# Linear attention beside a gated feed-forward, fp32 on one core: operands of the first key round loaded two feature blocks sooner, the first loads of w2 spread, and the last queries' sums put into rounds 1 and 2 of down

## The chip, the cores and the metric

The kernel runs on one core of a Trainium2 chip. The core has five engines that run beside each other, each with its own queue of instructions: TensorE (PE, with its weight loads apart as PEld), VectorE (DVE), ScalarE (ACT), GpSimd (POOL) and SyncE (SP). SP and ACT also ask for DMA transfers. The metric is the device time of one execution in microseconds (us), lower is better.

## The reference, cut to what matters

x is 2048 rows of 1024. It is normalized without parameters; two branches read the normalized xn. One is linear attention with 32 heads of 32, with a feature map of two softmaxes; the other is a gated feed-forward with 3584 features. Everything is fp32.

```python
xn = (x - mean) / sqrt(var + 1e-5)
q, k, v = split_heads(xn @ wqkv)
phi(t) = concat(softmax(t @ w_phi), softmax(-(t @ w_phi)))   # per head, over 32
kv = phi(k)^T v ;  z = sum over s of phi(k)
s = (phi(q) kv / (phi(q) z + 1e-6)) @ wo
g = silu((silu(xn @ w1) * (xn @ w3)) @ w2)
out = x + s * g
```

## The kernel before

**Products.** Every large matrix product is done by blocks with seven products in place of eight (Strassen's scheme in Winograd's form). The seven operands on one side are called A11, A12, S2, S1, S3, S4 and A22, those on the other B11, B21, T2, T1, T3, B22 and T4; the products run in the order of this list (ORDER), each named by its A operand. An fp32 operand is kept as a high part (a cast, ACT L93) and a low part (what the cast left over, DVE L94), and a product takes three passes (high x high, high x low, low x high). So a product of the gate and up, key and query stages is 12 matmuls of 128x512, and one of down 6.

**Stages.** Gate and up (L667) run over two halves of the rows (tb) and 28 feature blocks (f) of seven products (j = 0 to 6). Then come eight rounds for keys and eight for values (L930), eight query rounds (L1004; pos is their number, and the last of them is query_last), down (L1400), which multiplies the hidden features h by w2, and the output (L1554).

**Operands and loads.** The x operands of the key and query rounds (xo) lie in DRAM, each 512 KB per round, and reload() brings them back; wkv are the weights' operands, 2 MB each (op2B, op2T). The tiles of xo, the split weights of gate and up (bo) and the operands of down (hr, and the high and low parts af and as) share one pool of eleven buffers that is called q. Loads stand on SP's queue in the order in which the program writes them, mixed with the stores of h. The hidden features h are finished by DVE in each feature block and stored to h_d by SP. w2's operands go through a ring of 22 slots (load_b; the tiles are bo again), of which eight are there in the query rounds; two halves of 512 KB make one operand.

**Around the opening of down.** query_last computes the last pair of query blocks and prepares down's first operands between its products: first_parts makes A11 and A12 (af, cast and low part), and S2 (as2, which is made from sm, a sum of two parts of hr), second_parts makes the other four. The feature map of a query block is three steps (query_features): the maxima and the shifted values on DVE and GpSimd (ranged, L971 to L974), the exponential on ACT (raised, L977) that is stored by a transfer from ACT's queue (e_d), and the sums on DVE (summed, L982 to L984). What query_last doesn't finish it returns as a list of steps, and down runs it between its first products: a "piece" with number n is run behind product n of the rounds, 7 to a round.

**Down's rounds.** A round r works on one pair (kb, i): kb is a stretch of 512 features, i one of eight row groups. It runs A11, A12 and S2 of its own pair, mixed with S1, S3, S4 and A22 of the pair before. For kb = 0 the results are copied to acc by ACT (L1406) or added by DVE (L1414). A11 and S2 of one pair share a bank (bankb), which ACT has to have copied after A11 before S2 may start. gen1 is the generator that prepares the first operands of the next round, gen2 that of the other four of this one.

Of the kernel before, what the change touches and what calls it, by code (L numbers as in the profile page):

```python
# [28 lines left out]
def tile_kernel(ctx: ExitStack, tc: tile.TileContext, x, wkT, wqT, wv, wphi, wo, w1, w3, w2, out):  # L29
# [270 lines left out]

    in_order(ENG.PE, ENG.Activation, ENG.DVE, ENG.Pool, ENG.SP)
    ao, xs = {n: slot(0, j) for j, n in enumerate(ANAMES) if n in ("A11", "A12", "S2", "S1")}, []
    late_x = big.tile([P, 4, 2, 512], F, name="late_x", tag=f"big{HOMES[0][6]}")
    room_a = big.tile([P, 8, 4, P], F, name="room_a", tag=f"big{HOMES[0][5]}")
    room_b = big.tile([P, 8, 4, P], F, name="room_b", tag=f"big{HOMES[0][4]}")

    def load_tile(t, r):
        nc.sync.dma_start(r.rearrange("p u n -> p (u n)"), x[t * P:(t + 1) * P, :])
# [329 lines left out]
    def gate_up(step):  # L638
# [39 lines left out]
        def read():  # L678
# [37 lines left out]
            else:  # L716
# [11 lines left out]
                    del kept_banks[f]  # L728
                del banks[tb, f], bos[tb, f], bank
                h0 = u0 = u1 = h1 = None  # L730
            if last and tb:
                xo.update(reload(0, [ANAMES[0], ANAMES[1]] if j == 0 else ANAMES[j + 1:j + 2]))
            if last and (j < 5 if tb else 0 < j < 6):
                early.update(fetch(tb + 1, j + 1 + tb))
            if last and j == 6:
# [278 lines left out]
    def query_last(i, xo, wb):  # L1014

        bank, rho, q, feats, late = {}, small.tile([P, 2, 2, 16], F, name="rho"), {}, {}, []
        parts = first_parts(ahead.pop(0))

        def kept(n, pb):
            q[n] = work.tile([P, 512], F, name="q", tag="w")  # L1020
            nc.scalar.copy(q[n], pb)

        def added(n, pb, j, c, room):
            nc.vector.tensor_add(q[n], pb, q[n])
            feats[n] = query_features(i, j, c, q.pop(n), rho, nc.gpsimd, room, True)
            feats[n][0]()

        for b, an, bn in ORDER:
            pb = query_product(bank, b, an, bn, xo, wb)
            if an == "A11":  # L1030
                kept("00", pb)
                ahead[1] = load_h(0, 1)
            elif an == "A12":
                early = e_room()
                added("00", pb, 0, 0, early[:, 0])
                next(parts)
            elif an == "S2":
                kept("01", pb)
                feats["00"][1]()
                feats["00"][2]()  # L1040
                ready.append(next(parts))
                parts = second_parts(*ready[0])
            elif an == "S1":
                kept("11", pb)
                next(parts)
            elif an == "S3":
                added("11", pb, 1, 1, early[:, 1])
                next(parts)
            elif an == "S4":
                room = e_room()  # L1050
                added("01", pb, 0, 1, room[:, 0])
                feats["11"][1]()
                ready.append(next(parts))
                feats["11"][2]()
            else:
                feats["10"] = query_features(i, 1, 0, pb, rho, nc.vector, room[:, 1], True)
                feats["10"][0]()
        late.append(lambda: (feats["01"][1](), feats["01"][2]()))
        late.append(lambda: feats["10"][1]())
        late.append(lambda: (feats["10"][2](), rho_out(i, rho), feats.clear()))  # L1060
        return late

    def query_heads(i, first, xo, wb, steps):

# [70 lines left out]

    bos = {}

    def load_b(kb, n):
        n = BNAMES[n]
        for kk in range(2):  # L1140
            t = ring("bo")
            nc.sync.dma_start(t.bitcast(F), w2_d[kb][n][:, kk])
            bos[kb, n, kk] = t
# [50 lines left out]
    for c in range(3):  # L1194
# [5 lines left out]
        for pos, i in enumerate(order):  # L1200
            nxt, end = {}, pos + 1 == len(pairs)

            def steps():
                halves = []
                for j in range(7):
                    if not last:
                        wo_split(c, pos, j, halves)
                    if j == 0:
                        if pos in (3, 4) and not last:
                            wbn.update(fetch(3 + c, pos - 3))  # L1210
                        if not end:
                            nxt.update(reload(order[pos + 1]))
                        if last and 0 < pos < 5:
                            load_b(0, pos - 1)

                    if end and j in NEXT[c]:
                        wbn.update(fetch(3 + c, NEXT[c][j]))
                    if last and pos + 2 == len(pairs) and j == 5:
                        ahead[0] = load_h(0, 0)
                    yield  # L1220
# [230 lines left out]
    for k, do in enumerate((scale, scale, turn_e, turn_e)):  # L1451
        piece(7 * (50 + k // 2 * 2) + 5 + k % 2, lambda k=k, do=do: do(0, k % 2))
    old, banks, first, second = None, {}, ready[0], None
    for k, do in enumerate(late_features):
        piece(1 + 2 * k, do)
    late_features = None
    for r, new in enumerate(steps):
        kb, i = new or (NKB, 8)
# [2 lines left out]
            load_b(kb + 1, i - 2)  # L1461
        if r + 2 < len(steps) - 1:
            ahead[r + 2] = load_h(*steps[r + 2])
        if r == 2:
            late_rw.append(rwp.tile([P, 2, 2, 512], R, name="late", tag="rw"))
            room_z = rwp.tile([P, 2, D], F, name="room", tag="rw")
            zb, er = room_z[:, 0], room_z[:, 1]
# [12 lines left out]
        parts, bank = first, {}  # L1480
        if r and new:
            gen2 = second_parts(*parts)
        if r + 1 < len(steps) - 1:
            gen1 = first_parts(ahead.pop(r + 1))
        if kb and new:
            seed(i, bank, r)
        for m, (b, an, bn) in enumerate(TURN):
# [6 lines left out]
                    late_slots(bn)  # L1494
            if m < 3 and r and new:
                then = next(gen2)
            if m in (3, 4) and r + 1 < len(steps) - 1:
                first = next(gen1)
            if end and m in (1, 4) and 1 < i:
                gate(i - 2, m // 4)  # L1500
# [8 lines left out]
                do()  # L1509
        if new:  # L1510
            second = then if r else ready[1]
        old, banks = new, bank
    assert not pieces
    xrs = [slot_f("xr") for _ in range(2)]
# [130 lines left out]
```

## Time and profile before

| | |
|---|---|
| median of three runs | 2367.42 us (2367.08 to 2367.56) |
| the profiled execution, own time | 2366.58 us |
| its span in the trace | 2364.8 us |
| instructions | 37648 |
| DMA moved | 579.08 MB, mean 245 GB/s |

Times in the views are us from the start of the span. The page lists, for each engine, the time in which it was busy; PE was busy nearly all of the span, so the views that say more are the waits of PE, which list by cause each time PE stood still, and the timeline, where a row gives start, duration, engine, line and operation as "out<-in", with the idle time ahead of it and what ended that in brackets. The windows give the busy time of every engine, the clock that TensorE was granted (1 is full speed) and the use of the DMA engines in a stretch of time.

### The profile page before, as it was taken

How to read it: one execution, taken by the hardware profiler on the slowest of the kernel's cores; microseconds unless marked ns; L12 is line 12 of the kernel's file. 1: busy time of each engine (PE TensorE's matmuls, PEld its weight loads, DVE VectorE, ACT ScalarE, POOL GpSimd, SP SyncE). 2: the span in 40 equal slices, each digit the busy share in tenths (PEclk: the TensorE clock that was granted, in tenths of full speed). 3: DMA queues.
4: the chain of work that ended last, by engine and by line, in shares of the span. 5: the costliest groups of instructions: out<-in, count | busy, mean ns of one | idle time of the engine just before them, and what ended most of it. 6: DMA issues, size and time to landing. Idle time of an engine off the chain costs nothing.

```text
span 2364.8 us, 37648 instructions
## 1 busy us (share of the span) xinstructions
PE 2338.3 (99%) x14640; PEld 1916.5 (81%) x14640; DVE 1777.7 (75%) x2809; ACT 892.8 (38%) x1575; POOL 256.8 (11%) x213
## 2 busy tenths in 40 slices
PE   8999999999999999999999999999999999999999
PEld 6788877788888888888788888787888888888887
DVE  8877788875688888874566666777678888786775
ACT  6445444443355554443221222334433333352000
POOL 1000000000000000000000000331012222213562
PEclk9999999999999999999999999999999999999999
DMA  3556799997788988875978868986444553479763
GB/s 127 162 190 231 241 312 369 344 310 230 241 273 304 305 293 301 288 259 191 365 275 298 305 231 329 362 299 232 161 134 143 205 178 134 156 248 278 211 178 104
DMA packets 301490, 579.08 MB, mean 245 GB/s; under 512 B 24432, under 2 KB 156672, under 8 KB 298624
## 3 DMA queue, kind: packets, MB, share of 16 engines
q1 hardware_dynamic: 294976, 553.60, 69.3%
q10 hardware_dynamic: 6336, 23.07, 2.5%
q8 instruction: 115, 1.88, 0.3%
q14 instruction: 63, 0.52, 0.1%
HBM read 373.69 MB, written 202.91 MB: 244 GB/s over the span
## 4 chain that ended last, share of the span: by engine, by line
PE 95%; DMA 3%; DVE 1%; ACT 1%; issue 0%; SPq 0%; ACTq 0%
PE bankb L667 25%; PE bankb L1400 13%; PE bankc L667 12%; PE pm L1554 8%; PE bankb L930 7%; PE bankc L1400 6%; PE banka L667 6%; PE bankc L930 3%; PE bankb L1004 3%; PE banka L1400 3%; PE bankc L1004 2%; PE banka L930 2%; PE po L1539 1%; DMA xoA<-xo_d0A 1%; PE pkv L907 1%; PE banka L1004 1%
## 5 line engine op out<-in xcount | busy, mean ns | idle before, releaser
L94 DVE TENSOR_TENSOR bo<-rw,bo 128x512 fp32r<-128x512 f32 x329 | 226.1, 688 | 145.3 <-ACT bo L93 145.1
L1400 PE MATMUL bankb<-bo,as 128*128 128x512 f32 x960 | 236.3, 391 | 0.0
L1400 PEld LDWEIGHTS bankb<-bo,as 128*128 128x128 f32 x960 | 181.1, 189 | 37.7
L93 ACT CAST bo<-rw 128x512 fp32r<-128x512 f32 x329 | 202.3, 618 | 19.3 <-ACT wkvo L93 2.9
L667 PE MATMUL bankb<-op0S,bo 128*128 128x512 f32 x672 | 165.7, 396 | 4.5 <-ACT u L703 2.8
L667 PE MATMUL bankc<-op0S,bo 128*128 128x512 f32 x672 | 162.1, 390 | 0.0
L667 PE MATMUL bankb<-op1S,bo 128*128 128x512 f32 x672 | 161.3, 389 | 0.0
L667 PE MATMUL bankc<-op1S,bo 128*128 128x512 f32 x672 | 161.3, 389 | 0.0
L667 PE MATMUL bankb<-op0A,bo 128*128 128x512 f32 x672 | 159.3, 391 | 1.2 <-ACT op0A L765 0.8
L1554 PE MATMUL pm<-wos,oT 128*128 128x512 f32 x672 | 160.0, 393 | 0.0
L1400 PE MATMUL bankc<-bo,as 128*128 128x512 f32 x624 | 158.4, 389 | 0.0
L667 PE MATMUL bankb<-op1A,bo 128*128 128x512 f32 x672 | 157.9, 390 | 0.0
L667 PEld LDWEIGHTS bankb<-op0S,bo 128*128 128x128 f32 x672 | 125.6, 189 | 37.1 <-issue 5.3
L667 PEld LDWEIGHTS bankb<-op1A,bo 128*128 128x128 f32 x672 | 125.8, 188 | 28.1 <-DVE u L711 2.1
L667 PEld LDWEIGHTS bankb<-op0A,bo 128*128 128x128 f32 x672 | 125.4, 188 | 27.6 <-ACT op0A L765 1.1
L667 PEld LDWEIGHTS bankc<-op0S,bo 128*128 128x128 f32 x672 | 125.6, 188 | 27.3 <-issue 1.2
L667 PEld LDWEIGHTS bankc<-op1S,bo 128*128 128x128 f32 x672 | 126.2, 188 | 26.2
L667 PEld LDWEIGHTS bankb<-op1S,bo 128*128 128x128 f32 x672 | 126.2, 188 | 26.2
L1554 PEld LDWEIGHTS pm<-wos,oT 128*128 128x128 f32 x672 | 124.8, 188 | 27.4 <-DVE oT L1545 0.3
L1400 PEld LDWEIGHTS bankc<-bo,as 128*128 128x128 f32 x624 | 117.2, 188 | 24.4
L1414 DVE TENSOR_TENSOR acc<-bankb,acc 128x512 f32<-128x512 f32 x152 | 102.0, 685 | 32.7 <-PE bankb L1400 32.7
L718 ACT ACTIVATE h<-bankb 128x512 f32<-128x512 f32 x56 | 33.5, 598 | 239.7 <-PE bankb L667 239.5
(290 smaller groups left out, 4305.3 us busy)
## 6 DMA issues: line engine op xcount, KB each, us to landing
rw<-in_w SPq DMA_DIRECT2D x112, 512.0 KB, 4.9
hr<-h_d SPq DMA_DIRECT2D x56, 512.0 KB, 4.7
h_d<-h SPq DMA_DIRECT2D x108, 256.0 KB, 5.6
xoS<-xo_d0S SPq DMA_DIRECT2D x44, 512.0 KB, 7.2
xoS<-xo_d1S SPq DMA_DIRECT2D x44, 512.0 KB, 6.7
xoA<-xo_d0A SPq DMA_DIRECT2D x33, 512.0 KB, 5.3
xoA<-xo_d1A SPq DMA_DIRECT2D x33, 512.0 KB, 5.3
e_d<-eq ACTq DMA_DIRECT2D x32, 512.0 KB, 6.5
```

The costliest lines, as they stand in the source:

```text
L93: nc.scalar.copy(hi, src)
L94: (by or nc.vector).tensor_sub(lo, src, hi.bitcast(F))
L667: nc.tensor.matmul(bank[b], bos[tb, f][bn][:, w, k], ao[an][:, u, k], start=first and n == 0, stop=LAST[b] == an and n == 11, skip_group_c ...
L718: nc.scalar.activation(h1, bank["b"], AF.Silu)
L907: nc.tensor.matmul(pkv[sl, m], e[m // 4][:, (m % 4) * P + 32 * h:(m % 4) * P + 32 * h + 32], v[:, 4 * (m % 4) + h], start=first and m == 0 ...
L930: nc.tensor.matmul(bank[b], xo[an][:, u, k], wb[bn][:, w, k], start=an in ("A11", "A12", "S1") and n == 0, stop=LAST[b] == an and n == 11, ...
L1004: nc.tensor.matmul(bank[b], xo[an][:, u, k], wb[bn][:, w, k], start=an in ("A11", "A12", "S1") and n == 0, stop=LAST[b] == an and n == 11, ...
L1400: nc.tensor.matmul(bank[b], t[:, u, pos + k], bos[kb, bn, k][:, w], start=first and n == 0, stop=LAST[b] == an and n == 5, skip_group_chec ...
L1414: nc.vector.tensor_add(c, pb, c)
L1539: nc.tensor.matmul(po[32 * j:32 * j + 32, a, 64 * k:64 * k + 64], kvs[sl, j, c, k], et[sl, :, 4 * k + j], start=True, stop=True, skip_grou ...
L1554: nc.tensor.matmul(p, oTs[t, h][:, a, k], wos[c, 4 * h + k][:, b], start=n == 0, stop=n == 3 * ND - 1)
```

## The change

Four edits, and one exchange of lines:

- The x operands of the first key round are asked for in the last two feature blocks: A11, A12 and S2 in block 26 (products 4, 5 and 6), S1 and S3 with block 27's product 0, S4 and A22 with its products 3 and 4. Before, A11 and A12 were asked for with product 0 of block 27 and one more with each product after it.
- query_last makes the first operands of round 1, too (behind S4 and A22), and round 0 of down no longer does. The sums of query block 11 go from query_last into down; steps of the features move to pieces 1, 3 and 5 (round 0), 12 (round 1) and 19 (round 2, with the store of rho). The room that those features used is taken over for late w2 slots in round 4, not in round 2.
- The two halves of each of w2's first four operands are asked for at steps 2 and 5 of a query round, not both at step 0.
- Three rooms of the first stage are allocated in another order, so room_b has other addresses beside them.

```diff
--- before.py
+++ after.py
@@ -300,9 +300,9 @@
 
     in_order(ENG.PE, ENG.Activation, ENG.DVE, ENG.Pool, ENG.SP)
     ao, xs = {n: slot(0, j) for j, n in enumerate(ANAMES) if n in ("A11", "A12", "S2", "S1")}, []
+    room_b = big.tile([P, 8, 4, P], F, name="room_b", tag=f"big{HOMES[0][4]}")
     late_x = big.tile([P, 4, 2, 512], F, name="late_x", tag=f"big{HOMES[0][6]}")
     room_a = big.tile([P, 8, 4, P], F, name="room_a", tag=f"big{HOMES[0][5]}")
-    room_b = big.tile([P, 8, 4, P], F, name="room_b", tag=f"big{HOMES[0][4]}")
 
     def load_tile(t, r):
         nc.sync.dma_start(r.rearrange("p u n -> p (u n)"), x[t * P:(t + 1) * P, :])
@@ -728,8 +728,9 @@
                     del kept_banks[f]
                 del banks[tb, f], bos[tb, f], bank
                 h0 = u0 = u1 = h1 = None
-            if last and tb:
-                xo.update(reload(0, [ANAMES[0], ANAMES[1]] if j == 0 else ANAMES[j + 1:j + 2]))
+            if tb and f >= NF - 2:
+                xo.update(reload(0, {(0, 4): ANAMES[:1], (0, 5): ANAMES[1:2], (0, 6): ANAMES[2:3], (1, 0): ANAMES[3:5],
+                                     (1, 3): ANAMES[5:6], (1, 4): ANAMES[6:]}.get((f - NF + 2, j), ())))
             if last and (j < 5 if tb else 0 < j < 6):
                 early.update(fetch(tb + 1, j + 1 + tb))
             if last and j == 6:
@@ -1051,14 +1052,15 @@
                 added("01", pb, 0, 1, room[:, 0])
                 feats["11"][1]()
                 ready.append(next(parts))
-                feats["11"][2]()
+                parts = first_parts(ahead.pop(1))
+                next(parts)
             else:
+                ready.append(next(parts))
                 feats["10"] = query_features(i, 1, 0, pb, rho, nc.vector, room[:, 1], True)
                 feats["10"][0]()
-        late.append(lambda: (feats["01"][1](), feats["01"][2]()))
-        late.append(lambda: feats["10"][1]())
-        late.append(lambda: (feats["10"][2](), rho_out(i, rho), feats.clear()))
-        return late
+        return {1: lambda: feats["11"][2](), 3: lambda: feats["01"][1](), 5: lambda: feats["10"][1](),
+                7 + 5: lambda: feats["01"][2](),
+                14 + 5: lambda: (feats["10"][2](), rho_out(i, rho), feats.clear())}
 
     def query_heads(i, first, xo, wb, steps):
 
@@ -1135,9 +1137,9 @@
 
     bos = {}
 
-    def load_b(kb, n):
+    def load_b(kb, n, parts=range(2)):
         n = BNAMES[n]
-        for kk in range(2):
+        for kk in parts:
             t = ring("bo")
             nc.sync.dma_start(t.bitcast(F), w2_d[kb][n][:, kk])
             bos[kb, n, kk] = t
@@ -1210,9 +1212,8 @@
                             wbn.update(fetch(3 + c, pos - 3))
                         if not end:
                             nxt.update(reload(order[pos + 1]))
-                        if last and 0 < pos < 5:
-                            load_b(0, pos - 1)
-
+                    if last and 0 < pos < 5 and j in (2, 5):
+                        load_b(0, pos - 1, (j // 3,))
                     if end and j in NEXT[c]:
                         wbn.update(fetch(3 + c, NEXT[c][j]))
                     if last and pos + 2 == len(pairs) and j == 5:
@@ -1451,8 +1452,8 @@
     for k, do in enumerate((scale, scale, turn_e, turn_e)):
         piece(7 * (50 + k // 2 * 2) + 5 + k % 2, lambda k=k, do=do: do(0, k % 2))
     old, banks, first, second = None, {}, ready[0], None
-    for k, do in enumerate(late_features):
-        piece(1 + 2 * k, do)
+    for k, do in late_features.items():
+        piece(k, do)
     late_features = None
     for r, new in enumerate(steps):
         kb, i = new or (NKB, 8)
@@ -1461,7 +1462,7 @@
             load_b(kb + 1, i - 2)
         if r + 2 < len(steps) - 1:
             ahead[r + 2] = load_h(*steps[r + 2])
-        if r == 2:
+        if r == 4:
             late_rw.append(rwp.tile([P, 2, 2, 512], R, name="late", tag="rw"))
             room_z = rwp.tile([P, 2, D], F, name="room", tag="rw")
             zb, er = room_z[:, 0], room_z[:, 1]
@@ -1480,7 +1481,7 @@
         parts, bank = first, {}
         if r and new:
             gen2 = second_parts(*parts)
-        if r + 1 < len(steps) - 1:
+        if 0 < r < len(steps) - 2:
             gen1 = first_parts(ahead.pop(r + 1))
         if kb and new:
             seed(i, bank, r)
@@ -1494,7 +1495,7 @@
                     late_slots(bn)
             if m < 3 and r and new:
                 then = next(gen2)
-            if m in (3, 4) and r + 1 < len(steps) - 1:
+            if m in (3, 4) and 0 < r < len(steps) - 2:
                 first = next(gen1)
             if end and m in (1, 4) and 1 < i:
                 gate(i - 2, m // 4)
@@ -1509,6 +1510,9 @@
                 do()
         if new:
             second = then if r else ready[1]
+            if r == 0:
+                first = ready[2]
+                ready.clear()
         old, banks = new, bank
     assert not pieces
     xrs = [slot_f("xr") for _ in range(2)]
```

In the changed kernel line numbers from L735 on are one to four higher. How the order moves on SP's queue at the first key round. xo are the x operands, op2T and op2B the weights' operands. From A12's load on, before:

```order
L630 DMA xoA_9715<-xo_d0A_88 128x1024
L170 DMA op2T_9717<-wkv_d1T_110 128x4096
L630 DMA xoS_9737<-xo_d0S_89 128x1024
L170 DMA op2T_9739<-wkv_d1T_111 128x4096
L623 DMA h_d_6_70<-h_9581 128x4x128
L630 DMA xoS_9759<-xo_d0S_90 128x1024
L170 DMA op2T_9761<-wkv_d1T_112 128x4096
L630 DMA xoS_9778<-xo_d0S_91 128x1024
L170 DMA op2B_9780<-wkv_d1B_113 128x4096
L630 DMA xoS_9795<-xo_d0S_92 128x1024
L170 DMA op2T_9797<-wkv_d1T_114 128x4096
L630 DMA xoA_9813<-xo_d0A_93 128x1024
```

and after the change:

```order
L630 DMA xoA_9679<-xo_d0A_88 128x1024
L630 DMA xoS_9699<-xo_d0S_89 128x1024
L630 DMA xoS_9719<-xo_d0S_90 128x1024
L630 DMA xoS_9721<-xo_d0S_91 128x1024
L170 DMA op2T_9723<-wkv_d1T_110 128x4096
L170 DMA op2T_9743<-wkv_d1T_111 128x4096
L623 DMA h_d_6_70<-h_9581 128x4x128
L170 DMA op2T_9763<-wkv_d1T_112 128x4096
L630 DMA xoS_9780<-xo_d0S_92 128x1024
L170 DMA op2B_9782<-wkv_d1B_113 128x4096
L630 DMA xoA_9797<-xo_d0A_93 128x1024
L170 DMA op2T_9799<-wkv_d1T_114 128x4096
```

S2, S1 and S3 (xoS, of d0S_89, 90 and 91) stand ahead of the first two weights' operands now; S4 and A22 one weight operand sooner than before.

How it moves on ACT's queue at the opening of down. as<-s is a cast of round 0's second operands, af<-hr and as<-sm those of round 1's first ones, COPY acc<-bankb the copy of a product of down, and eq and e_d are the exponentials of the query features and their store. Before:

```order
L93 CAST as<-s_14353 128x512
L1406 COPY acc<-bankb 128x512
L977 ACTIVATE eq<-eq 128x1024
L978 DMA e_d_204<-eq 128x1024
L93 CAST af<-hr 128x512
L977 ACTIVATE eq<-eq 128x1024
L978 DMA e_d_208<-eq 128x1024
L93 CAST as_14446<-sm 128x256
L1406 COPY acc<-bankb 128x512
```

and after the change:

```order
L93 CAST as<-s_14353 128x512
L93 CAST af<-hr 128x512
L93 CAST as_14381<-sm 128x256
L1407 COPY acc<-bankb 128x512
L978 ACTIVATE eq<-eq 128x1024
L979 DMA e_d_204<-eq 128x1024
L1407 COPY acc<-bankb 128x512
L978 ACTIVATE eq<-eq 128x1024
L979 DMA e_d_208<-eq 128x1024
L1407 COPY acc<-bankc 128x512
```

The two casts of round 1's operands, af and the small one from sm, stand ahead of the first COPY of acc; before they stood behind it.

And on DVE's queue in the same place, from the low part of round 0's operand as on. r and rho are the sums of the features, mm the maxima of the last query block. Before:

```order
L94 TENSOR_TENSOR as<-s_14353,as 128x512
L982 TENSOR_REDUCE r<-eq 128x32
L983 RECIPROCAL rho<-r 128x16
L984 TENSOR_TENSOR rho<-r,rho 128x16
L971 TENSOR_REDUCE mm_14395<-bankb 128x16
L972 TENSOR_REDUCE mm_14395<-bankb 128x16
L973 TENSOR_TENSOR eq<-bankb,mm_14395 128x512
L974 TENSOR_TENSOR eq<-mm_14395,bankb 128x512
L982 TENSOR_REDUCE r<-eq 128x32
L983 RECIPROCAL rho<-r 128x16
L984 TENSOR_TENSOR rho<-r,rho 128x16
L1414 TENSOR_TENSOR acc<-banka,acc 128x512
```

and after the change:

```order
L94 TENSOR_TENSOR as<-s_14353,as 128x512
L1158 TENSOR_TENSOR sm<-hr 128x256
L94 TENSOR_TENSOR af<-hr,af 128x512
L94 TENSOR_TENSOR as_14381<-sm,as_14381 128x256
L972 TENSOR_REDUCE mm_14399<-bankb 128x16
L973 TENSOR_REDUCE mm_14399<-bankb 128x16
L974 TENSOR_TENSOR eq<-bankb,mm_14399 128x512
L975 TENSOR_TENSOR eq<-mm_14399,bankb 128x512
L983 TENSOR_REDUCE r<-eq 128x32
L984 RECIPROCAL rho<-r 128x16
L985 TENSOR_TENSOR rho<-r,rho 128x16
L1415 TENSOR_TENSOR acc<-banka,acc 128x512
```

sm and the two low parts of round 1 stand right behind the low part of as, where the sums of block 11 stood; these sums now come behind the last block's shifted values.

## The prediction

> **What bounds the kernel now.** I read the page first, then the waits of PE, then the timeline where each wait lies.
>
> ```profile
> PE 2338.3 (99%) x14640; PEld 1916.5 (81%) x14640; DVE 1777.7 (75%) x2809; ACT 892.8 (38%) x1575; POOL 256.8 (11%) x213
> ```
>
> PE sets the time, and the change neither adds nor removes a matmul, so it can only gain where PE waits or runs at a slow clock. The waits of PE by cause (total, times, longest, in us):
>
> ```profile
> PE bankb L1400 <- DVE af L94: 3.4, 1, 3.4
> PE bankb L930 <- DMA xoA<-xo_d0A: 3.2, 1, 3.2
> PE bankb L667 <- ACT u L703: 2.8, 1, 2.8
> PE bankc L1004 <- ACT q L1070: 1.2, 1, 1.2
> ```
>
> The first, second and fourth lie at the three places that the diff touches: the opening of down, the first key round, and the query round that loads w2. The third is at the start of the kernel; the change leaves it alone, but it shows what an idle stretch does to the clock.
>
> **What the first key round loses.** The timeline there (start, duration, engine, line, operation, and in brackets the idle time before it and who ended it):
>
> ```profile
> 1119.09 2.88 PE L930 MATMUL bankb<-op2B,xoA 128*128 128x512 f32 x12
> 1121.81 2.88 PE L930 MATMUL banka<-op2B,xoA 128*128 128x512 f32 x12
> 1139.25 5.46 PE L930 MATMUL bankb<-op2T,xoA 128*128 128x512 f32 x12 [3.20 <-DMA xoA<-xo_d0A]
> 1147.61 2.88 PE L930 MATMUL banka<-op2B,xoA 128*128 128x512 f32 x12
> ```
>
> The first two rows start 2.72 apart: one product. The last row is eight products behind the first, so without loss it would start 21.76 later; it starts 28.52 later. The loss is 6.76: 3.2 of it idle ahead of A22's product (the seventh), most of the rest a slow clock, which the windows show (us, length, five engines' busy time, PE clock, DMA share, GB/s):
>
> ```profile
> 1086.00:1103.00 17.00, 17.00 (x77) 14.08 (x76) 9.69 (x15) 5.53 (x11) 0.13 (x1) 1.00 0.20 63
> 1103.00:1118.00 15.00, 15.00 (x68) 12.43 (x67) 4.15 (x6) 3.38 (x6) 0.13 (x1) 1.00 0.93 349
> 1118.00:1136.00 18.00, 17.79 (x78) 14.14 (x76) 7.95 (x11) 4.59 (x6) 0.00 (x0) 1.00 1.02 430
> 1139.00:1142.00 3.00, 2.75 (x7) 2.21 (x8) 0.00 (x0) 0.10 (x1) 0.00 (x0) 0.50 1.07 396
> 1142.00:1146.00 4.00, 4.00 (x12) 3.16 (x11) 1.25 (x3) 0.52 (x1) 0.00 (x0) 0.59 1.03 421
> ```
>
> The transfers are the cause: full at 430 GB/s from 1118, and nearly unused, at 63, in the 17 us before 1103.
>
> **Part 1, the operands sooner.** What fills the full stretch, from the DMA view of 1080 to 1140 (count, KB each, median us to landing), and the chain's piece that ends the wait:
>
> ```profile
> op2T<-wkv_d1T SPq DMA_DIRECT2D x4, 2048.0 KB, 16.2
> xoS<-xo_d0S SPq DMA_DIRECT2D x7, 512.0 KB, 13.1
> h_d<-h SPq DMA_DIRECT2D x7, 256.0 KB, 12.4
> wo_raw<-in_wo SPq DMA_DIRECT2D x1, 256.0 KB, 5.8
> ...
> 1117.77 21.34 DMA xoA<-xo_d0A
> ```
>
> In SP's order S2, S1 and S3 now stand ahead of T2, and are asked for at steps that begin at 1097 and 1100, in the unused stretch (block 27 begins seven products, 19.04, before 1119.09, and block 26 ends with the step before). So three times 512 KB, 1.57 MB, leave the stretch that is full. The A22 operand landed at 1117.77 + 21.34 = 1139.11; at 430 GB/s 1.57 MB are 3.66, so the last landing of the round moves to 1135.45. A22's product is due at 1119.09 + 6 x 2.72 = 1135.41: its wait is gone to within 0.3, and the slow clock behind it with it. What is late next is the A11 operand of round 2: on SP it stands behind three stores of h and wo_raw, and 0.79 + 0.26 + 0.52 MB at 430 are 3.66 after T4, 1139.1, against a product due at 1138.1. That leaves 1.0 idle. Its following operands come every 1.2, a product takes 2.72, so it is the only one. The bounds: 0 if the stretch is served a little faster, and 2.3 if its 17 us ran at the 396 of the fourth window instead of 430 (1.3 more). I take 1.0, since the same bytes at the same queue depth ran at 430 there: gain 5.8, between 4.5 and 6.8. Taking the quads for these operands sooner costs nothing as long as eleven suffice for them and for the weights of the last two blocks together; the order puts no new wait ahead of a cast there.
>
> **Part 2, the opening of down.** The rows around it:
>
> ```profile
> 1608.31 1.05 POOL L973 TENSOR_TENSOR eq<-q,mm 128x512 f32<-128x512 f32 x1 [5.18 <-DVE mm L971]
> 1608.74 0.90 DVE L1168 TENSOR_TENSOR s<-hr,sm 128x256 f32<-128x256 f32 x1
> ...
> 1611.36 1.52 PE L1400 MATMUL bankb<-bo,af 128*128 128x512 f32 x6
> ...
> 1612.04 0.63 ACT L93 CAST as<-s 128x512 fp32r<-128x512 f32 x1 [0.40 <-ACT eq L977]
> ...
> 1612.70 1.27 DVE L94 TENSOR_TENSOR as<-s,as 128x512 fp32r<-128x512 f32 x1
> ...
> 1612.92 0.59 ACT L1406 COPY acc<-bankb 128x512 f32<-128x512 f32 x1 [0.25 <-PE bankb L1400]
> 1613.38 1.50 POOL L974 TENSOR_TENSOR eq<-mm,q 128x512 f32<-128x512 f32 x1
> ...
> 1614.08 1.52 PE L1400 MATMUL bankb<-bo,as 128*128 128x512 f32 x6
> ...
> 1620.13 0.41 DVE L1156 TENSOR_TENSOR sm<-hr 128x256 f32<-128x256 f32 x1
> ...
> 1620.58 0.41 ACT L93 CAST as<-sm 128x256 fp32r<-128x256 f32 x1 [1.50 <-DVE sm L1156]
> ...
> 1621.20 2.08 PE L1400 MATMUL bankb<-bo,af 128*128 128x512 f32 x4 [3.42 <-DVE af L94]
> ...
> 1627.44 1.55 PE L1400 MATMUL bankc<-bo,as 128*128 128x512 f32 x6
> ```
>
> A product is 1.36 (two of them from 1611.36 to 1614.08). From the first PE row to the last are seven products, 9.52, and they took 16.08: a loss of 6.56. 3.4 of it is the wait on af for round 1's first product, whose low part stands on DVE behind the sums and reduces of the last query tiles. The rest is mostly the slow clock behind that wait:
>
> ```profile
> 60.00:64.00 4.00, 3.47 (x9) 2.29 (x7) 3.86 (x7) 1.77 (x4) 0.00 (x0) 0.60 0.04 9
> 1525.00:1530.00 5.00, 3.67 (x16) 2.55 (x15) 2.09 (x4) 1.80 (x3) 0.00 (x0) 1.00 1.02 392
> 1530.00:1534.00 4.00, 4.00 (x19) 3.28 (x18) 2.82 (x5) 0.85 (x1) 2.06 (x2) 1.00 1.03 412
> 1621.00:1624.00 3.00, 2.80 (x7) 2.25 (x8) 2.93 (x8) 2.06 (x4) 0.00 (x0) 0.50 0.85 295
> 1624.00:1627.00 3.00, 3.00 (x10) 2.35 (x9) 1.50 (x4) 1.17 (x2) 0.00 (x0) 0.58 0.86 254
> ```
>
> The change puts sm, the low part of af and that of the first sum (as2) ahead of the last tile's reduces, right behind the low part of round 0's as (the row of 1612.70). So af is whole near 1616 instead of 1621.1, and the wait of 3.4 is gone. But ACT's two casts of round 1 now stand ahead of the COPY of round 0's first product, and that COPY frees bankb for round 0's third product, the row of 1614.08. The second of the casts needs sm. DVE is free for sm at 1612.70 + 1.27 = 1613.97; GpSimd's L974 runs from 1613.38 to 1614.88. The row of 1608.74 shows what comes of that: a 128x256 operation with two operands took 0.90 beside GpSimd, against 0.41 for the same size alone at 1620.13; and L974 itself took 1.50, ending 0.9 after DVE's as. I read it as one after the other: sm ends at 1614.88 + 0.41 = 1615.3, the cast (0.41) at 1615.7, the COPY (0.59) at 1616.35. The third product starts there instead of at 1614.08: **a new wait of 2.3**. Bounds: 1.4 if sm runs at once, 2.8 if it takes 0.90 behind GpSimd. Behind it nothing new is late: round 1's first product comes at 1619, well after af; the sums that were put into rounds 1 and 2 run on a DVE that is 75% busy, and the last store of rho with them, which only the next two loads of w2 stand behind.
>
> What the clock makes of 2.3 idle is not shown. An idle time of 2.8 (u L703, quoted above) was followed by the window 60 to 64 at 0.60, which costs 4 x 0.40 = 1.6; one of 1.2 (q L1070) lies in 1525 to 1530, and the clock stayed at 1.00. Between these two ends, 0 and 1.6, I take the middle, 0.8. So 3.1 of the 6.56 stay (1.4 to 4.4): gain 3.4, between 2.1 and 5.2.
>
> [...]
>
> **Part 3, w2's loads.** The query round with pos 1:
>
> ```profile
> 1522.35 2.88 PE L1004 MATMUL bankc<-op4T,xoS 128*128 128x512 f32 x12
> ...
> 1528.94 0.58 ACT L1070 COPY q<-bankc 128x512 f32<-128x512 f32 x1 [2.73 <-DMA bo<-w_d0T]
> ...
> 1532.48 2.88 PE L1004 MATMUL bankb<-op4T,xoA 128*128 128x512 f32 x12
> ```
>
> Three products took 10.13 instead of 8.16: 1.97 lost, since ACT waited for a transfer of w2 and PE for ACT's copy. In SP's order only the first pair of these loads moves, behind the stores of kv and z; every other load keeps its place, because the loop that issues them runs in the same SP order with or without the spread. I put it at 0; the bounds are 0 and 1.97 gained. The exchanged rooms change only which address a tile has, and one buffer's release; the rows show PE waiting on none of them: 0. Raising the late rooms from round 2 to round 4 costs nothing, as their first use is behind round 4.
>
> **The sum.** 5.8 + 3.4 + 0 = 9.2. The profiled execution took 2366.58, of which the span is 2364.8; 9.2 less is 2357.4. The median of the runs, 2367.42, lies 0.84 above that execution, so the forecast for the median is **2358.2**. With all bounds at their best 12.0 is gained, 2355.4; at their worst 6.6, 2360.8.
>
> **The rivals.** *The opening gives most of its gain back.* The new wait comes to 2.8 and the clock falls as after the old one: the windows 1621 to 1624 at 0.50 and 1624 to 1627 at 0.58 cost 3 x 0.50 + 3 x 0.42 = 2.8. Then 5.6 of 6.56 stay, the gain is 0.9 + 5.8 = 6.7, and the time 2360.7. For it: ACT serves its queue in order, and the COPY stands behind two casts. Against: 2.3 is the reading nearest to the rows, and the clock has a chance to hold.
>
> [...]
>
> *The spread works after all*: the 1.97 of pos 1 go too, 11.2 gained, 2356.2. Against: in that round neither the loads nor what they stand behind has moved.
>
> *The earlier operands don't lighten the full stretch*: SP asks for them late, because the transfers ahead of them hold it up, and T2 queues behind them. The round then loses its 6.76 again, only the 3.4 are gained, 2364.0. Against: 63 GB/s in the 17 us before 1103 leaves room for all.
>
> *Slower: the quads run short.* Operands and the halves of gate and up's weights share eleven quads. If the earlier loads take those that the last products' weights need, each of the ten products from the fifth of block 26 on waits until a quad is free and then for its preparation, a cast of 0.63 (row of 1612.04) and a low part, 0.69 on average:
>
> ```profile
> L94 DVE TENSOR_TENSOR bo<-rw,bo 128x512 fp32r<-128x512 f32 x329 | 226.1, 688 | 145.3 <-ACT bo L93 145.1
> ```
>
> Ten times 1.32 are 13.2, less 9.2: 4.0 slower, 2371.4. It decides if fewer quads stay for the weights than are in use at once. For it: one kernel-wide pool feeds both, and DVE waits 145 us on casts. Against: I count at most ten in use.
>
> **Chances.** The forecast 0.50 (its own range 2355.4 to 2360.8); the clock holds 0.10; the spread works 0.07; the opening gives back 0.18; the full stretch stays 0.08; the quads run short 0.07. 0.2% is 4.7 us, about what a measurement of this kernel tells from no change. Below 2362.7 lie the first four, 0.85 faster; the stretch at 2364.0 counts as same, 0.08; the quads as slower, 0.07. The range: from 2355.0, a little below the best bounds, to 2362.5, above the opening's rival; the last two cases, 0.15, are left out.
>
> **What would show it.** Right: no wait of PE on an xo operand above 0.5 in the first key round, a clock of 1.00 from 1139 to 1146, and about 1 us idle at the first product of round 2. In the opening no wait on af, and one of 1.4 to 2.8 at round 0's third product, on ACT's COPY of acc; the window behind it shows the clock. In pos 1 the wait on q stays. Wrong: PE waiting on a weight half (bo) in blocks 26 and 27; SP asking for S1 and S3 only after 1103; or the wait on A22 of 3 us still there.

## The result, and the profile after

| | before | after |
|---|---|---|
| median of four runs | 2367.49 us (2367.08 to 2369.08) | 2356.78 us (2354.42 to 2357.06) |
| ratio | | 0.9959, 95% interval 0.9947 to 0.9971 |
| the profiled execution, own time | 2366.58 us | 2356.99 us |
| its span | 2364.8 us | 2355.2 us |

The forecast for the median was 2358.2 (2355.0 to 2362.5). By the ratio 9.7 us are gained (6.9 to 12.5), by the medians 10.7; 9.2 were forecast. The profiled executions differ by 9.6. The first line of the page's busy times after:

```profile
PE 2332.2 (99%) x14640; PEld 1912.7 (81%) x14640; DVE 1779.1 (76%) x2809; ACT 893.1 (38%) x1575; POOL 256.2 (11%) x213
```

PE is 6.1 less busy with the same 14640 matmuls: a matmul at a slow clock counts as busy (A22's product in the first key round 5.46 before, with the clock at 0.50, and 2.88 now), so that much of the gain is slow clock, the rest idle time. The waits of PE after (total, times, longest), the rows that are new or changed:

```profile
PE bankc L1005 <- ACT q L1072: 2.1, 1, 2.1
PE bankb L1401 <- ACT acc L1407: 1.9, 1, 1.9
...
PE bankb L931 <- DMA xoA<-xo_d0A: 0.5, 1, 0.5
```

The waits of 3.4 on af and of 3.2 on A22's operand are gone; the new one on ACT's copy of acc, and the smaller one at round 2's first key product, are those that the prediction named. The first key round after, in the timeline:

```profile
1119.03 2.88 PE L931 MATMUL bankb<-op2B,xoA 128*128 128x512 f32 x12
...
1135.35 2.88 PE L931 MATMUL bankb<-op2T,xoA 128*128 128x512 f32 x12
...
1138.77 3.01 PE L931 MATMUL bankb<-op2B,xoA 128*128 128x512 f32 x12 [0.54 <-DMA xoA<-xo_d0A]
...
1141.62 2.88 PE L931 MATMUL banka<-op2B,xoA 128*128 128x512 f32 x12
```

From first to last row are 22.59 against 21.76 for eight products: 0.83 lost where 6.76 were. The windows (length, busy times of five engines, clock, DMA share, GB/s) show why:

```profile
1086.00:1103.00 17.00, 17.00 (x77) 14.08 (x76) 9.63 (x15) 5.59 (x11) 0.13 (x1) 1.00 0.51 153
1103.00:1118.00 15.00, 15.00 (x68) 12.43 (x67) 4.15 (x6) 3.33 (x6) 0.13 (x1) 1.00 0.96 376
1118.00:1136.00 18.00, 18.00 (x81) 14.91 (x80) 8.40 (x12) 4.59 (x6) 0.00 (x0) 1.00 1.02 407
1138.00:1142.00 4.00, 3.46 (x16) 2.70 (x15) 3.08 (x5) 0.85 (x2) 0.00 (x0) 1.00 1.03 421
```

The 17 us before 1103 carry 153 GB/s instead of 63: 90 GB/s in 17 us are 1.53 MB, close to the 1.57 of the three operands. The stretch behind is as full as before: from 1103 to 1136 13.0 MB are moved in both kernels (349 x 15 + 430 x 18 against 376 x 15 + 407 x 18), so the loads that follow have moved up by those 1.5 MB. The clock stays at 1.00. The opening of down after:

```profile
1606.16 1.52 PE L1401 MATMUL bankb<-bo,af 128*128 128x512 f32 x6
...
1608.17 1.50 POOL L975 TENSOR_TENSOR eq<-mm,q 128x512 f32<-128x512 f32 x1
1608.69 1.27 DVE L1158 TENSOR_TENSOR sm<-hr 128x256 f32<-128x256 f32 x1
...
1609.99 0.40 ACT L93 CAST as<-sm 128x256 fp32r<-128x256 f32 x1 [2.01 <-DVE sm L1158]
1610.30 0.58 ACT L1407 COPY acc<-bankb 128x512 f32<-128x512 f32 x1
...
1610.93 1.65 PE L1401 MATMUL bankb<-bo,as 128*128 128x512 f32 x6 [1.89 <-ACT acc L1407]
...
1617.86 1.52 PE L1401 MATMUL bankc<-bo,as 128*128 128x512 f32 x6
```

The reader can follow the chain backwards: PE waits for ACT's COPY, the COPY stands behind the cast of as, the cast waits 2.01 for sm, and sm took 1.27 beside GpSimd's L975, where 0.41 is its time alone. Seven products took 11.70 instead of 9.52, so 2.18 stay of 6.56. The windows of this place:

```profile
1608.00:1611.00 3.00, 1.11 (x6) 0.61 (x4) 3.00 (x5) 1.01 (x3) 1.67 (x2) 1.00 0.73 289
1611.00:1614.00 3.00, 3.00 (x13) 2.48 (x14) 3.00 (x5) 2.11 (x3) 0.00 (x0) 1.00 0.50 184
```

Behind the wait the clock is at 1.00 here. The round of the query stage that waits for ACT's copy of q (the rows from its fourth to its seventh product):

```profile
1523.42 0.33 ACTq L979 DMA_DIRECT2D e_d<-eq  x1
1523.79 0.58 ACT L1072 COPY q<-bankc 128x512 f32<-128x512 f32 x1 [3.56 <-DMA bo<-w_d0T]
1524.43 3.02 PE L1005 MATMUL bankc<-op4B,xoS 128*128 128x512 f32 x12 [2.06 <-ACT q L1072]
```

It lost 1.97 before and 2.35 now, all of it idle; the window behind the wait is at full clock:

```profile
1525.00:1530.00 5.00, 5.00 (x23) 4.13 (x22) 3.67 (x6) 1.06 (x1) 2.94 (x3) 1.00 1.01 382
```

So the accounts of these two profiles close: 5.93 in the key round and 4.38 at the opening, less 0.38 here, are 9.93, against 9.6 in the span.

### The profile page after: what moved, and what is told of

The parts are those of the page before. It is cut to its first block, busy times and chain, and to the rows that moved or that the text cites. A ratio compares the mean times of both kernels' runs of the same rounds, so it can differ in the third digit from the quotient of the medians.

```text
span 2355.2 us, 37653 instructions
## 1 busy us (share of the span) xinstructions
PE 2332.2 (99%) x14640; PEld 1912.7 (81%) x14640; DVE 1779.1 (76%) x2809; ACT 893.1 (38%) x1575; POOL 256.2 (11%) x213
## 3 DMA queue, kind: packets, MB, share of 16 engines
q8 instruction: 115, 1.88, 0.3%
## 4 chain that ended last, share of the span: by engine, by line
PE 94%; DMA 2%; DVE 2%; ACT 1%; SPq 1%; issue 0%; POOL 0%; ACTq 0%; POOLq 0%; DVEq 0%
PE bankb L667 26%; PE bankb L1401 13%; PE bankc L667 13%; PE pm L1558 8%; PE bankb L931 7%; PE bankc L1401 6%; PE banka L667 6%; PE bankc L931 4%; PE banka L1401 3%; PE bankb L1005 2%; PE banka L931 2%; PE bankc L1005 1%; PE po L1543 1%; PE pkv L908 1%; DMA xoA<-xo_d0A 1%; PE banka L1005 1%
```

## The experiments

Each run left a profile, and the three losses can be read from each as above (first key round over eight products, opening of down over seven, waiting query round over three). "Beside" is the median of the kernel before, measured together with it on the same chip.

| kernel | median | beside | ratio (95%) | key | opening | query |
|---|---|---|---|---|---|---|
| before (first profile) | 2367.49 | | | 6.76 | 6.56 | 1.97 |
| the change | 2356.78 | 2367.49 | 0.9959 (0.9947 to 0.9971) | 0.83 | 2.18 | 2.35 |
| operands sooner alone | 2360.33 | 2365.84 | 0.9976 (0.9965 to 0.9987) | 0.96 | 5.69 | 1.88 |
| query_last alone | 2364.03 | 2365.84 | 0.9989 (0.9980 to 0.9998) | 6.44 | 3.78 | 2.35 |
| w2 spread alone | 2365.18 | 2365.84 | 0.9996 (0.9987 to 1.0006) | 5.50 | 6.94 | 1.21 |
| rooms alone | 2365.83 | 2365.84 | 0.9998 (0.9989 to 1.0007) | 5.11 | 5.53 | 1.97 |
| new order, not sooner | 2362.17 | 2366.33 | 0.9981 (0.9972 to 0.9991) | 1.18 | 5.59 | 2.54 |
| a block sooner still | 2357.94 | 2366.33 | 0.9967 (0.9954 to 0.9979) | 0.00 | 2.20 | 1.28 |
| the change again | 2356.63 | 2366.40 | 0.9962 (0.9950 to 0.9975) | 0.73 | 3.80 | 1.40 |
| copy first | 2354.95 | 2366.40 | 0.9954 (0.9941 to 0.9966) | 1.68 | 0.00 | 2.39 |
| w2 last | 2356.30 | 2366.40 | 0.9958 (0.9944 to 0.9971) | 0.64 | 3.79 | 0.00 |
| copy first and w2 last | 2353.48 | 2366.40 | 0.9947 (0.9935 to 0.9960) | 1.11 | 0.00 | 0.00 |

**The operands sooner, alone.**

```diff
-            if last and tb:
-                xo.update(reload(0, [ANAMES[0], ANAMES[1]] if j == 0 else ANAMES[j + 1:j + 2]))
+            if tb and f >= NF - 2:
+                xo.update(reload(0, {(0, 4): ANAMES[:1], (0, 5): ANAMES[1:2], (0, 6): ANAMES[2:3], (1, 0): ANAMES[3:5],
+                                     (1, 3): ANAMES[5:6], (1, 4): ANAMES[6:]}.get((f - NF + 2, j), ())))
```

> The kernel before with the sooner loads of the x operands alone. My theory (three operands leave the full stretch of transfers): the first key round's loss falls from 6.76 to about 0.8 us, so 5.9 less, 2361.5; in the trace no wait of PE on A22's operand, one of about 0.5 at round 2's first product, and the opening of down loses its 6.6 as before. Rival (the room order or w2's loads share in it): the wait on A22's operand stays in part, and less than 4 us are gained.

The theory held: key loss 0.96, the wait of 3.4 on af at the opening as before, 5.5 under the median beside it. This edit alone carries more than half of the gain.

**query_last alone.**

```diff
-                feats["11"][2]()
+                parts = first_parts(ahead.pop(1))
+                next(parts)
             else:
+                ready.append(next(parts))
                 feats["10"] = query_features(i, 1, 0, pb, rho, nc.vector, room[:, 1], True)
...
-        if r + 1 < len(steps) - 1:
+        if 0 < r < len(steps) - 2:
             gen1 = first_parts(ahead.pop(r + 1))
...
```

> The kernel before with the change to query_last and down's first rounds alone. Theory: the opening's loss falls from 6.56 to about 2.2 us, 4.4 less, 2363.0; PE's wait on af is gone and one of 1.9 on ACT's copy of acc stands at round 0's third product. Rival (the clock falls behind such a wait, and held in the changed kernel by chance): the same wait, then a window at about 0.6, and only 2 to 3 us gained, 2364.5 to 2365.5.

Here the rival was right in this run. The wait is the same 1.89, but behind it the windows show another clock than in the changed kernel:

```profile
1613.00:1616.00 3.00, 1.11 (x5) 0.65 (x4) 3.00 (x5) 1.24 (x3) 1.45 (x1) 1.00 0.98 317
1616.00:1619.00 3.00, 3.00 (x9) 2.28 (x9) 3.00 (x5) 1.24 (x3) 0.00 (x0) 0.51 0.78 321
```

At 0.51 the products are slow and the opening's loss is 3.78, 1.6 more than in the changed kernel's first profile with the same wait. The gain is only just clear of the noise (the interval ends at 0.9998): 1.8 by the medians and 2.6 by the ratio, instead of 4.4.

**w2's spread alone.** load_b gets the halves that it has to load as an argument, and its calls move:

```diff
-                        if last and 0 < pos < 5:
-                            load_b(0, pos - 1)
+                    if last and 0 < pos < 5 and j in (2, 5):
+                        load_b(0, pos - 1, (j // 3,))
```

> The kernel before with the spread of w2's first loads alone. Theory: SP's order hardly moves, so nothing: 2367.4 within 0.7, and the wait on ACT's copy of q in the fourth query round stays at 1.2 to 2.1. Rival (the spread does relieve the transfers, and the changed kernel hides it): that wait gone, 2365.5.

No difference that can be measured. The wait on the copy of q stands at 0.9, a loss of 1.21. In the five profiles without the spread this round loses 1.88 to 2.54; in the five with it and with these loads in their place, 1.21 to 1.40 three times and 2.35 to 2.39 twice. Whether the spread helps in a part of the executions stays open; the median doesn't show it.

**The rooms alone.** The line of room_b moved ahead of late_x, nothing else.

> The kernel before with the exchanged order of the three rooms alone. Theory: only addresses change, 2367.4 within 0.7, the waits of PE the same as before. Rival (another release of the buffer helps a load of the second stage): one of the waits shorter, up to 1.5 us gained.

No difference either. Note its key loss of 5.11 and opening of 5.53, each over 1 us less than in the first profile of before, with the same waits (3.2 and 3.4): that is the clock again (0.51 and 0.94 in the windows 1139 to 1142 and 1142 to 1146, where it was 0.50 and 0.59), and a single profile must not be read as a gain of an edit.

**The new order, but nothing asked for before block 27.** Written on the kernel before:

```diff
-                xo.update(reload(0, [ANAMES[0], ANAMES[1]] if j == 0 else ANAMES[j + 1:j + 2]))
+                xo.update(reload(0, {0: ANAMES[:5], 3: ANAMES[5:6], 4: ANAMES[6:]}.get(j, ())))
```

> The kernel before with the new order of the first key round's loads, but none asked for before block 27: A11, A12, S2, S1 and S3 with its product 0, S4 and A22 with its products 3 and 4. SP's order of loads is that of the changed kernel. Theory (time counts: bytes have to leave the full stretch for the unused one ahead of it): the stretch starts at 1100 as before and holds the same bytes, A22's product waits 2 to 3.2 us again, and at most 1.5 us are gained. Rival (order counts: it is enough that S2, S1 and S3 stand ahead of T2): the wait is gone as in the changed kernel, 5.5 gained.

My theory fell, and the rival was right in its mechanism: the wait is gone and the key loss is 1.18. The time is 4.2 under the one beside it, not 5.5; the intervals of this run and of the operands sooner alone overlap. SP's queue tells why. Before (start, duration, queue, line, transfer):

```profile
1086.67 3.05 SPq L630 DMA_DIRECT2D xoA<-xo_d0A  x2
1102.96 0.32 SPq L170 DMA_DIRECT2D op2T<-wkv_d1T  x1
1103.38 0.37 SPq L630 DMA_DIRECT2D xoS<-xo_d0S  x1
```

and in this kernel:

```profile
1089.96 0.33 SPq L630 DMA_DIRECT2D xoA<-xo_d0A  x1
1092.69 5.71 SPq L630 DMA_DIRECT2D xoS<-xo_d0S  x3
1103.52 3.04 SPq L170 DMA_DIRECT2D op2T<-wkv_d1T  x2
```

Before, A11 and A12 were asked for at 1086.67, though the program puts them with a product that begins at 1100: SP was 13 us ahead of the matmuls there, as far as its waits let it. Then T2's load stood still until 1102.96, and S2 behind it. The waits of SP's queue from 1085 to 1125 name the cause, before:

```profile
SPq L170 <- PE bankb L667: 14.4, 2, 13.1
```

A weights' load waited 13.1 for a matmul, the last reader of the room it goes into. With S2, S1 and S3 ahead of T2, they don't wait behind it, though the program puts them into block 27. The time does count, but it is the order that gives it: the 17 us before 1103 carry 162 GB/s in this kernel, too. The change puts no load of the key round into the program more than three products sooner, not two blocks, as the title of this text reads; what that adds can't be told from these runs: 0.96 against 1.18, where kernels with the loads of the change lose 0.64 to 1.68.

**A block sooner still.** The change with NF - 3 in place of NF - 2.

> The changed kernel with all the first key round's loads another block sooner (from product 4 of block 25 on). Theory (eleven quads just suffice for the change's timing): two or three more are held while the last two blocks' weights need theirs, so casts of bo come late and PE waits on bo in blocks 26 and 27: 3 us or more slower than the changed kernel, though the wait of 0.5 at round 2's first product goes. Rival (there is room for more): no wait on bo, and 0.5 to 1 us under the changed kernel.

The quads don't run short: no wait on bo, and the key round loses nothing at all:

```profile
1068.00:1086.00 18.00, 18.00 (x81) 14.88 (x81) 10.66 (x17) 6.26 (x12) 0.00 (x0) 1.00 0.66 228
1086.00:1103.00 17.00, 17.00 (x77) 14.08 (x76) 9.46 (x15) 5.46 (x10) 0.13 (x1) 1.00 0.28 85
```

Five of the seven operands are asked for from 1072.80 to 1080 now. Yet the median isn't better than the change's; the profile lost 1.6 more at the kernel's start, on a tile of x (3.1 there instead of 1.5), which the edit doesn't touch. Whether it is a gain of 0.8 stays open.

That start tells something of the clock. The first row is the kernel before, the second this one:

```profile
58.87 4.60 PE L667 MATMUL bankb<-op0S,bo 128*128 128x512 f32 x12 [2.84 <-ACT u L703]
58.65 3.01 PE L667 MATMUL bankb<-op0S,bo 128*128 128x512 f32 x12 [2.84 <-ACT u L703]
```

Behind the same idle time the product is slow in one and at full speed in the other. In eleven of the twelve profiles on record the clock falls here, and only in this one it holds; so the 2.8, by which the prediction reckoned the clock, is no sure case either.

**The change again.**

> The changed kernel once more, on the chip of the next three. Theory (the wait on ACT's copy of acc always stands at 1.9, and whether the clock falls behind it is chance): the wait is 1.9 again; the window behind it is at 1.00 or near 0.5, and the time 9 to 10 us or 7.5 to 8.5 us under the kernel before. Rival (the clock always holds behind a wait of 1.9 in this kernel): 1.00 again, over 9 us under the kernel before.

The same kernel, the same wait, and this time a slow clock behind it:

```profile
1608.00:1611.00 3.00, 2.82 (x9) 2.25 (x10) 3.00 (x6) 1.78 (x4) 0.00 (x0) 0.70 0.40 132
1611.00:1614.00 3.00, 3.00 (x11) 2.37 (x10) 1.73 (x5) 1.96 (x3) 0.00 (x0) 0.73 0.97 229
```

The opening's loss is 3.80 instead of 2.18. So the clock behind this wait isn't the same in every execution of one kernel: the opening's loss is 2.18 and 2.20 in two profiles (the change, a block sooner) and 3.78 to 3.80 in three (this one, query_last alone, w2 last): it held twice and fell three times, at 1.6 each time. The theory held, and the rival is refuted. The profiles come from more than one chip, but the chip alone doesn't decide it, as far as the mean clock of a run tells. In the profiled executions of the change and its variants that is 0.999 where the clock held and 0.998 where it fell. The five runs of this kernel on one chip have 0.999 three times and 0.998 twice, and all ten of copy first and of both edits, which lack that wait, have 0.999. What decides it stays open.

The time didn't go by the clock alone: this execution is 9.8 under the median beside it, where the theory gave 7.5 to 8.5 for a slow clock; its query round lost 1.40, not 2.35.

**ACT's copy first.** In the changed kernel, the first sum of round 1 is split behind round 0's first product:

```diff
             else:
-                ready.append(next(parts))
                 feats["10"] = query_features(i, 1, 0, pb, rho, nc.vector, room[:, 1], True)
                 feats["10"][0]()
-        return {1: lambda: feats["11"][2](), 3: lambda: feats["01"][1](), 5: lambda: feats["10"][1](),
+        return {1: lambda: (ready.append(next(parts)), feats["11"][2]()), 3: lambda: feats["01"][1](), 5: lambda: feats["10"][1](),
```

> The changed kernel, with the cast and low part of round 1's first sum (as2) made behind round 0's first product, so that ACT's copy of acc stands ahead of that cast. Theory (the copy waits for the cast, the cast for sm, sm for GpSimd): the wait of 1.9 at round 0's third product goes, nothing else comes in its place, the opening's loss falls from 2.2 or more to under 0.5: 2 to 3.5 us under the changed kernel. Rival (the copy is late for another cause, ACT's exponentials or the sums on DVE): the wait stays above 1 us, or moves to round 1's first product.

The theory held for the wait. The opening in the timeline:

```profile
1606.19 1.52 PE L1400 MATMUL bankb<-bo,af 128*128 128x512 f32 x6
...
1607.92 0.58 ACT L1406 COPY acc<-bankb 128x512 f32<-128x512 f32 x1
...
1608.72 1.27 DVE L1157 TENSOR_TENSOR sm<-hr 128x256 f32<-128x256 f32 x1
1608.91 1.52 PE L1400 MATMUL bankb<-bo,as 128*128 128x512 f32 x6
...
1610.03 0.41 ACT L93 CAST as<-sm 128x256 fp32r<-128x256 f32 x1 [1.53 <-DVE sm L1157]
...
1615.71 1.52 PE L1400 MATMUL bankc<-bo,as 128*128 128x512 f32 x6
```

sm is as slow as before, and its cast as late, but the copy doesn't stand behind it; seven products take 9.52 exactly. The median is 1.7 under the change's beside it, where 2 to 3.5 were expected, and the two sets of five runs overlap (2353.64 to 2356.42 against 2354.83 to 2359.63).

**w2's third and fourth operand in the last query round.** In the changed kernel:

```diff
                 ahead[1] = load_h(0, 1)
+                load_b(0, 2)
+                load_b(0, 3)
...
-                    if last and 0 < pos < 5 and j in (2, 5):
+                    if last and 0 < pos < 3 and j in (2, 5):
```

> The changed kernel, with the third and fourth operand of w2 (T2 and T1, 2 MB) asked for in the last query round instead of the fourth and fifth. Theory (the stores of e on ACT's queue wait for loads in transfers that are full at 400 GB/s, and the copy of q behind them): without 2 MB in that stretch the wait of 1.2 to 2.1 on the copy of q in the fourth query round goes, 2 us under the changed kernel, and nothing waits for T2 or T1 at the opening. Rival (the e stores wait whatever stands in the stretch, or the later loads come too late): the wait stays, or PE waits on bo at the opening.

The wait on the copy of q is gone, and nothing waits for w2 at the opening. On ACT the store of e and the copy of that round stand right behind their exponential (which starts at 1518.21 and takes 1.06); in the change (first profile) the copy had 3.56 of idle time ahead of it:

```profile
1519.30 0.33 ACTq L979 DMA_DIRECT2D e_d<-eq  x1
1519.67 0.59 ACT L1074 COPY q<-bankc 128x512 f32<-128x512 f32 x1 [0.40 <-ACT eq L978]
```

So it is these 2 MB that make ACT's stores of e, and the copy behind them, late. The windows of the two query rounds, this kernel first and then the change again:

```profile
1489.00:1506.00 17.00, 17.00 (x77) 14.08 (x76) 13.45 (x25) 4.95 (x6) 5.13 (x5) 1.00 0.95 348
1506.00:1525.00 19.00, 19.00 (x86) 15.73 (x85) 14.86 (x26) 6.01 (x7) 6.16 (x7) 1.00 1.01 380
```

```profile
1489.00:1506.00 17.00, 17.00 (x77) 14.08 (x76) 13.16 (x24) 5.74 (x7) 5.25 (x6) 1.00 1.01 390
1506.00:1525.00 19.00, 17.90 (x80) 14.48 (x79) 13.79 (x24) 5.22 (x7) 5.94 (x6) 1.00 1.03 406
```

PE is busy for the whole stretch at 348 and 380 GB/s and stands still 1.1 at 390 and 406. The median is only 0.3 lower, which the spread of the runs doesn't tell from nothing; this profile has two other waits of 1.1 and 1.2 in the key and output stages.

**Both.**

> Both edits of the last two together. Theory: they add, 4 to 5.5 us under the changed kernel. Rival (the later loads of w2 collide with the opening, once its wait is gone): a wait on bo or hr in down's first rounds, and less than 3 us under the changed kernel.

The opening and the query round lose nothing, and the ratio to the kernel before is 0.9947: the fastest kernel of the study. The median is 3.2 under the change's beside it, less than the 4 to 5.5 of the theory. It is 2.8 under that of w2 last, and these two sets of runs don't overlap (2352.45 to 2354.63 against 2354.85 to 2357.63): so the copy put first does save time. From 1600 to 1900 the waits of PE list nothing in its profile, so it is no collision at the opening. What is there more of is a wait of the key rounds on ACT, which was 0.8 in the change's first profile:

```profile
PE bankc L931 <- ACT ev L952: 2.0, 2, 1.2
```

The edits needn't be what brings it: a block sooner, without them, had 1.5 there in two waits, and the change again had none. And the clock behind the opening's wait seems to cost the change its 1.6 only in a part of its runs, which would make the medians differ by less than these profiles.

## Why the prediction was right, point by point

- *The key round, 5.8 forecast:* 5.93 in the first profile, 5.8 in the run alone. The sum of bytes was right: 1.5 MB moved ahead, A22's wait gone, then round 2's first product late, 0.54 instead of 1.0, and no slow clock. One step of it was wrong in its mechanism. The prediction had S2, S1 and S3 "asked for at steps that begin at 1097 and 1100"; SP asked for them from 1089.36 to 1097.78, as it was ahead of PE, and what held them before was T2 at the head of SP's queue (13.1). The new place in the order is what gains; an earlier place in the program isn't needed for it, as the run with the new order alone showed.
- *The opening, 3.4 forecast:* 4.38 in the first profile, 2.8 in three others, from the 6.56 of before. The new wait, its place, its cause and its size (1.89 idle, 2.05 from start to start; 2.3 forecast) came as worked out, from the one row of 0.90 against 0.41. The 0.8 for the clock was a middle between 0 and 1.6, and the runs showed that both ends happen: 0 in two profiles and 1.6 in three. A mean of five is 1.0; so the value was right as a mean by luck, a middle taken for want of a row, and no single profile has it.
- *The sum, 9.2 forecast:* that it came within 0.5 of the 9.7 is partly luck. 6.76 is the highest key loss of the four profiles with that wait (5.11 to 6.76, mean 5.95), and 6.56 lies above the mean of the five with the wait on af (6.06). By the means on record the six profiles with the loads of the change gain 5.0 in the key round, and the five with the new wait 2.9 at the opening: 7.9, which the interval of 6.9 to 12.5 allows. The best bound of 12.0 leaves out the 1.97 that Part 3 itself allowed for.
- *The clock holds, a chance of 0.10:* the forecast's 0.8 for the clock is then not lost, 10.0 are gained, 2357.4. Of the five profiles with the new wait two show it and three don't; there 1.89 idle was followed by windows at 0.51 to 0.77. What decides between the two, no run here shows.
- *w2's spread, 0 forecast:* no difference measured (0.9987 to 1.0006); on SP only the first pair of these loads moves. The prediction named the round wrongly: it called it the one with pos 1. It is the fourth round, pos 3: five rounds of 19.04 and the 2.35 lost lie between its first product and the opening of down at 1606.16. pos 1 and pos 3 load different operands of w2. The argument holds there, too: in the run alone, SP asks for the loads around that round in the same order as before.
- *The rooms and late rooms, 0 forecast:* 0 for the rooms alone; the late rooms were run only together with query_last and left no wait.
- *The rivals.* The opening that gives most back (2360.7) didn't come in full: the wait was 1.89, not 2.8, but a fall of the clock, at 1.6 instead of 2.8, came in three of five profiles. The quads were not short even a block sooner, so its point of decision was further off than my count of ten suggested. The stretch that stays full, 2364.0, didn't come: SP asked in time. The stretch moved as many bytes as before, but it began 1.5 MB ahead.

## What to carry to other kernels

A load that waited 13.1 for its room held up the loads behind it on SP's queue here; order the loads by when their rooms come free, and look at the queue's own waits before moving a load to an earlier place in the program. When work is moved ahead on an engine, look at what it now stands in front of: here a cast whose input was late delayed a copy that freed PE's bank, and moving that cast behind the copy gave another 1.7 us by the medians, and 2.8 once the later w2 loads were in. The eight waits of PE of 1.89 to 2.25 cost 0.3 more than their own length here (2.18 for 1.89, 2.35 for 2.06), and three of them 1.6 us of slow clock in addition; so price such a wait with both, and compare medians, not single profiles.

## What the runs showed of the hardware

- The same wait of 1.89 to 1.90 was followed by a clock of 1.00 in two profiles and by a slow stretch in three (a window of 3 us at 0.51 in one, two at 0.66 to 0.77 in each of the others), at a price of 1.6 each time. Behind the waits on q of 2.06 to 2.25 the clock was at 1.00 in all three profiles, and the round lost 2.35 to 2.54. Behind the 2.79 to 2.85 at the kernel's start it fell in eleven of twelve (the product behind it took 4.60 in the kernel before, and 3.01 in the one profile where it held). Behind the waits of 3.1 to 3.4 in the key round and at the opening it fell each time, at a price that varied: the key round lost 5.1 to 6.8 with a wait that was the same within 0.1.
- Two operands on DVE beside GpSimd: sm of 128x256 took 1.27 when it started 0.98 before GpSimd's operation ended, and 0.41 alone.
- SP asked for transfers up to 13 us ahead of the product beside which the program has them (A11 and A12 from 1086.67, the product begins at 1100), and a load that waited 13.1 for its room held those behind it until 1103.
